# Attention state chained from PSUM, the first batch's norm in another order, and wider filler matmuls in a Trainium2 kernel

## The chip, the cores and the metric

The kernel runs on one core of one Trainium2 chip, as one launch. The metric is the device time of the launch in microseconds: the median of three runs of the kernel before is 517.42 us (517.26 to 517.53). Inside the core the engines work side by side: TensorE (PE in the profile; PEld is its loading of weights), VectorE (DVE), ScalarE (ACT), GpSimd (POOL), and SyncE (SP), which here issues DMA transfers. Each engine works through its own list of instructions in order; semaphores between them hold an instruction back until its inputs are there and its outputs' buffers are free.

## The reference

What is computed, for q, k, v, alpha of shape [4, 8, 768, 48] and two weight matrices, w_ch1 of 384x1536 and w_ch2 of 1536x384, all in float32:

```
for t in range(768):                       # per batch and head; state is 48x48
    state = alpha[t][:, None] * state + outer(k[t], v[t])
    y[t]  = q[t] @ state
x  = y of all heads side by side            # [4, 768, 384]
u  = x + real(fft(fft(x, axis=1), axis=2))  # over the sequence, then the channels
un = (u - mean(u)) / sqrt(var(u) + 1e-6)    # over the 384 channels
out = u + relu(un @ w_ch1) @ w_ch2
```

## The kernel before

One Python function, `gla_mix_ffn`, writes the whole program. It does not issue instructions at once: every call on V (VectorE), A (ScalarE), G (GpSimd), T (TensorE) is recorded in a `Plan` together with the tiles that it reads and writes, a key (its wished place) and whether it is marked low. The planner then goes through the recorded work by list scheduling, with a table of estimated durations, and writes down for each engine one fixed order. Ready work with the smallest key goes first, and work marked low may wait for a gap. The instructions are issued in that order by `emit`, so that nearly all of them carry one line number, L538 (L542 in the changed kernel); the ReLU carries L221 (L223).

The work comes in four batches. A batch has four **head pairs**, two heads side by side on 112 partitions (48 of the one, a gap, 48 of the other, which begins at `GRP` = 64). `attn_stages` writes each pair in eight stages. s1 turns alpha into running products within blocks of 128 tokens by two scans on VectorE (tiles `al`, `w`), s2 and s3 multiply k and q by them, s4 transposes k, s5 makes the masked product of q and k of each block (copied from PSUM by ScalarE, masked by GpSimd). **s6 makes the state that enters each block**: five TensorE products of k and v into one PSUM tile `pu` (five blocks of 96 columns), a multiplication of all 480 columns by `mh` on VectorE, which scales each block and zeroes the quarters that mix two heads, and then four chained `scalar_tensor_tensor` steps in the SBUF tile `tt`, each of them the state before times a factor `mt` plus the new block. `mh` comes from two ScalarE operations on `mt` and a half mask `hm`. s7 adds what the state gives to each block's output, s8 combines the blocks of tokens into `z` for the FFT.

`mix_stages` makes the two DFTs as matmuls: `mk_s(0..3)` over the sequence, `mk_d(0..2)` over the channels, each `mk_d` adding its result to one third of the first half of `u` (`us[0]`), and `fb` adding the same results, in mirrored order, to the second half (`us[1]`), whose rows `f0` has fetched in reversed order. `norm_stages` n1 computes mean and variance by `bn_stats` and `bn_aggr`, the root on ScalarE, one step of refinement on VectorE (tiles `r`), and scales on ScalarE; n2 transposes the result on TensorE and splits it into a high and a low part `x`. `ffn_stages` computes both products as three matmuls each (high by high, high by low, low by high), into `h` and then into the output. The weights are split in the same way by `wsplit(j)`, which loads a block and passes it through ScalarE, VectorE and GpSimd; `WS` names the scratch tile of each pair of blocks.

Attention and mixing of batch 0 come first, and there is no FFN to do beside them. Later the FFN of one batch runs beside the attention and mixing of the next one. Where the planner sees TensorE idle before a planned time of 120 us, it puts **filler matmuls** on a tile of zeros there, one for each 0.11 us of the gap; they write to a part of PSUM that nothing reads (L1251; a 32-column product of 32 rows). Both parts of a filler, weight load and matmul, stand in the profile; one filler makes two matmul records.

## Time and profile before

| | before |
|---|---|
| median of three runs | 517.42 us (517.26 to 517.53) |
| profiled execution, its own time | 517.73 us |
| its span | 516.0 us |
| TensorE busy | 501.2 us, 97% |
| of that, filler matmuls | 29.5 us, 696 records |
| VectorE busy | 334.8 us, 65% |
| ScalarE busy | 196.1 us, 38% |
| GpSimd busy | 65.6 us, 13% |

The profile shows one execution. The 1.7 us between span and time lie around the profiled program. A row of the timeline gives the start in us, the length, the engine, the line, the operation with the tile that it writes and those that it reads, the shapes, a count of instructions taken together, and in brackets how long the engine was idle before it and what released it. A row of the windows gives for a stretch its length and then the busy time of each engine with the count of instructions, and at the end the granted TensorE clock (1.00 is full speed), the busy share of the DMA engines and GB/s. Times of a group of matmuls reach to the end of the last one.

### The profile page before, as it was taken

How to read it: one execution, taken by the hardware profiler on the slowest of the kernel's cores; microseconds unless marked ns; L12 is line 12 of the kernel's file. 1: busy time of each engine (PE TensorE's matmuls, PEld its weight loads, DVE VectorE, ACT ScalarE, POOL GpSimd, SP SyncE). 2: the span in 40 equal slices, each digit the busy share in tenths (PEclk: the TensorE clock that was granted, in tenths of full speed). 3: DMA queues.
4: the chain of work that ended last, by engine and by line, in shares of the span. 5: the costliest groups of instructions: out<-in, count | busy, mean ns of one | idle time of the engine just before them, and what ended most of it. 6: DMA issues, size and time to landing. Idle time of an engine off the chain costs nothing.

```text
span 516.0 us, 9708 instructions
## 1 busy us (share of the span) xinstructions
PE 501.2 (97%) x3970; PEld 481.4 (93%) x3970; DVE 334.8 (65%) x729; ACT 196.1 (38%) x427; POOL 65.6 (13%) x86
## 2 busy tenths in 40 slices
PE   7999979999999999999999999999999999999995
PEld 7899868999999999999999999999999999999994
DVE  8889997997889996757799514656758213113112
ACT  4675467645663235443323214433123213111110
POOL 0312243022122000221100001112110000000000
PEclk9999998999999999999999999999999999999998
DMA  8990420422555101352431001120111001001001
GB/s 303 409 402 36 125 62 2 153 93 86 198 188 163 62 1 46 109 184 89 146 94 47 2 0 47 34 75 2 60 34 46 1 1 46 1 0 47 0 1 51
DMA packets 16978, 44.48 MB, mean 86 GB/s; under 512 B 1888, under 2 KB 7136, under 8 KB 16928
## 3 DMA queue, kind: packets, MB, share of 16 engines
q1 hardware_dynamic: 15872, 41.38, 22.5%
q0 software_dynamic: 768, 2.36, 1.6%
q8 instruction: 33, 0.54, 0.4%
q14 instruction: 17, 0.14, 0.1%
q10 hardware_dynamic: 288, 0.07, 0.1%
HBM read 36.72 MB, written 7.08 MB: 85 GB/s over the span
## 4 chain that ended last, share of the span: by engine, by line
PE 93%; DVE 3%; ACT 2%; issue 0%; ACTq 0%; DVEq 0%
PE f L538 63%; PE a L538 26%; PE f L1251 4%; DVE z L538 1%; DVE wt L538 1%; ACT wt L538 1%; ACT L538 0%; DVE y L538 0%; DVE r L538 0%; DVE f L538 0%; ACT x L538 0%; ACTq L538 0%; DVE w L538 0%; ACT b L538 0%; ACT f L538 0%
## 5 line engine op out<-in xcount | busy, mean ns | idle before, releaser
L538 PE MATMUL f<-wt,h 128*128 128x384 f32 x864 | 180.1, 344 | 0.3 <-ACT h L221 0.3
L538 PE MATMUL f<-x,wt 128*128 128x384 f32 x864 | 179.5, 345 | 0.0
L538 PEld LDWEIGHTS f<-x,wt 128*128 128x128 f32 x864 | 151.6, 189 | 1.3 <-issue 0.2
L538 PEld LDWEIGHTS f<-wt,h 128*128 128x128 f32 x864 | 150.7, 188 | 1.7 <-ACT h L221 0.4
L538 DVE SCALAR_TENSOR_TENSOR h<-f,h 128x384 fp32r<-128x384 f32 x96 | 53.2, 555 | 118.0 <-ACT h L221 117.2
L221 ACT ACTIVATE h<-f 128x384 fp32r<-128x384 f32 x96 | 47.0, 491 | 174.8 <-PE f L538 174.5
L538 POOL TENSOR_SCALAR_AFFINE_SELECT w<-w 128x384 f32<-128x384 f32 x48 | 30.1, 648 | 205.1 <-ACT w L538 143.3
L538 PE MATMUL a<-vn,w 128*128 128x64 f32 x288 | 41.2, 266 | 0.0
L538 ACT COPY w<-a 128x384 f32<-128x384 f32 (+4 forms) x60 | 26.6, 482 | 34.8 <-PE a L538 34.4
L538 PEld LDWEIGHTS a<-vn,w 128*128 128x128 f32 x288 | 39.4, 191 | 0.0
L1251 PEld LDWEIGHTS f<-zero 128*32 128x32 f32 x696 | 26.3, 119 | 7.7 <-ACT zero L538 3.3
L1251 PE MATMUL f<-zero 128*32 128x32 f32 x696 | 29.5, 203 | 3.8 <-ACT zero L538 3.3
L538 DVE TENSOR_TENSOR_SCAN w<-al,d 112x768 f32<-112x768 f32 (+1 forms) x17 | 28.4, 1670 | 4.8 <-PE a L538 4.7
L538 DVE TENSOR_TENSOR_SCAN al<-al,back 112x768 f32<-112x768 f32 (+1 forms) x17 | 28.2, 1660 | 0.0
L538 PE MATMUL a<-tt,w 112*128 112x96 f32 x144 | 28.0, 278 | 0.0
L538 PE MATMUL a<-w,al 48*128 48x128 f32 (+1 forms) x306 | 26.2, 290 | 0.0
L538 PEld LDWEIGHTS a<-w,al 48*128 48x128 f32 (+1 forms) x306 | 20.5, 187 | 5.1 <-issue 2.2
L538 PEld LDWEIGHTS a<-tt,w 112*128 112x128 f32 x144 | 23.4, 190 | 0.9
L538 DVE TENSOR_TENSOR y<-y,f 128x384 f32<-128x384 f32 (+2 forms) x36 | 18.5, 528 | 7.7 <-PE f L538 7.6
L538 DVE TENSOR_TENSOR y<-y,a 128x191 f32<-128x191 f32 (+5 forms) x66 | 21.0, 363 | 1.2 <-PE a L538 1.2
L538 ACT ACTIVATE c<-al,cm 128x781 uint8<-128x781 uint8 (+1 forms) x17 | 15.5, 912 | 14.7 <-DMA al<-in_chunked_dram 14.6
L538 DVE TENSOR_TENSOR z<-f 128x288 f32<-128x288 f32 (+3 forms) x40 | 21.1, 569 | 0.0
(120 smaller groups left out, 555.7 us busy)
## 6 DMA issues: line engine op xcount, KB each, us to landing
kq<-in_kq_dram SPq DMA_DIRECT2D x13, 768.0 KB, 6.0
wt<-in_w_dram SPq DMA_DIRECT2D x8, 768.0 KB, 7.9
al<-in_chunked_dram SPq DMA_DIRECT2D x15, 392.0 KB, 5.2
out_dram<-y SPq DMA_DIRECT2D x24, 192.0 KB, 1.9
vn<-in_v_dram SPq DMA_DIRECT2D x14, 296.0 KB, 3.7
wt<-in_w_dram SPq DMA_DIRECT2D x8, 384.0 KB, 7.2
scr<-y SPq DMA_DIRECT2D x4, 576.0 KB, 3.7
wt<-in_kq_dram SPq DMA_DIRECT2D x2, 768.0 KB, 10.0
```

Of the source, the lines that this page charges most:

```text
L221: return lambda out, x: e.activation(out, x, AF.Relu)
L538: op.ins = op.fns[op.engine](*[real(a) for a in op.args], **{k: real(x) for k, x in op.kwargs.items()})
L1251: plan.idle = (lambda: nc.tensor.matmul(warm[2][0:32, 480:512], zero.real(), zero.real(), start=True, stop=True), 1.0, WARM, ("f2", 2))
```

## The change

The change has four parts.

1. **State (s6).** The chain reads PSUM itself. ScalarE copies block 0 of `pu` to the new tile `tq`; each of the four `scalar_tensor_tensor` steps on VectorE computes the state before times `mt` plus a block of `pu`, into one of three places of `tq`. For each of the five blocks two ScalarE operations of 48x48, one for each head, write the state times `mt` to `tt`, the tile that TensorE reads. The quarters of `tt` that mix two heads are set to zero once, at the start, by GpSimd. `mh`, `hm`, the mask operations and the multiplication of 480 columns are gone.
2. **Norm of batch 0.** In batch 0 the norm of the first half is recorded ahead of `fb`, which is marked low there, as is the norm of the second half. The norm of the first half is made in two groups, thirds 0 and 1 together and third 2 alone. In all batches the refinement has fewer operations: the 1e-6 is added inside a `scalar_tensor_tensor`, and a `tensor_scalar` is replaced by such an operation as well.
3. **Fillers.** A planned gap of over 3.0 us is filled with matmuls of 128 columns, one for each 0.25 us; a shorter gap as before.
4. **Scratch.** The list `WS` now names wt6 to wt11 once each and then, in turn, `f` and `z`; `z` is taken when a batch first writes it. The splits 12 to 16 are recorded behind the first norm, with those from 18 on.

```diff
-WS = ('wt6', 'wt7', 'wt8', 'wt6', 'wt7', 'wt8', 'wt9', 'wt10', 'wt11', 'f', 'f', 'f')
+WS = ('wt6', 'wt7', 'wt8', 'wt9', 'wt10', 'wt11', 'f', 'z', 'f', 'z', 'f', 'z')
+FB0 = 11
-DUMMY = 0.11
+DUMMY = (0.11, 0.25)
+LONG = 3.0
...
-                for _ in range(int((t - max(clock["PE"], self.idle[1])) / DUMMY)):
-                    order.append(self.idle[0])
+                gap = t - max(clock["PE"], self.idle[1])
+                kind = gap > LONG
+                for _ in range(int(gap / DUMMY[kind])):
+                    order.append(self.idle[0][kind])
...
-            mh = mhs[i]
-            for hd in range(2):
-                A.activation(mh[0:CW, :, hd], mt[0:CW, 0 : NT - 1], AF.Copy, scale=hm[0:CW, hd : hd + 1])
-            V.tensor_tensor(
-                out=tt[0:CW], in0=pu[0:CW, 0 : (NT - 1) * 2 * D].rearrange("p (a h e) -> p a h e", h=2, e=D),
-                in1=mh[0:CW, :, :, None].broadcast_to([CW, NT - 1, 2, D]), op=ALU.mult,
-            )
-            for a in range(1, NT - 1):
-                V.scalar_tensor_tensor(
-                    out=tt[0:CW, a], in0=tt[0:CW, a - 1], scalar=mt[0:CW, a : a + 1], in1=tt[0:CW, a], op0=ALU.mult, op1=ALU.add,
-                )
+            past = None
+            for a in range(NT - 1):
+                now = pu[0:CW, a * 2 * D : (a + 1) * 2 * D]
+                if a:
+                    to = tq[0:CW, a % 3]
+                    V.scalar_tensor_tensor(out=to, in0=past, scalar=mt[0:CW, a - 1 : a], in1=now, op0=ALU.mult, op1=ALU.add)
+                    now = past = to
+                else:
+                    past = tq[0:CW, 0]
+                    A.copy(past, now)
+                for hd, r in ((0, slice(0, D)), (1, slice(GRP, CW))):
+                    A.activation(tt[r, a, hd], now[r, hd * D : (hd + 1) * D], AF.Copy, scale=mt[r, a : a + 1])
...
+            def scales(m0, m1):
+                for m in range(m0, m1):
+                    V.bn_stats(out=st[:, m], in_=u[:, m])
+                    V.bn_aggr(out=mv[:, m], in_=st[:, m])
+                mean, var, s, r, n = mv[:, m0:m1, 0], mv[:, m0:m1, 1], sq[:, m0:m1], r0[:, m0:m1], nm[:, m0:m1]
+                A.activation(s, var, AF.Sqrt, bias=ceps)
+                V.reciprocal(r, s)
+                V.tensor_mul(s, r, r)
+                V.scalar_tensor_tensor(out=s, in0=var, scalar=1e-6, in1=s, op0=ALU.add, op1=ALU.mult)
+                V.scalar_tensor_tensor(out=s, in0=s, scalar=0.5, in1=r, op0=ALU.mult, op1=ALU.mult)
+                V.scalar_tensor_tensor(out=r, in0=r, scalar=1.5, in1=s, op0=ALU.mult, op1=ALU.subtract)
+                V.scalar_tensor_tensor(out=n, in0=mean, scalar=-1.0, in1=r, op0=ALU.mult, op1=ALU.mult)
+                for m in range(m0, m1):
+                    A.activation(un[m], u[:, m], AF.Identity, bias=nm[:, m : m + 1], scale=r0[:, m : m + 1])
...
-            return st[:-1] + nst[:FB] + st[-1:] + nst[FB:]
+            return st[:-1] + nst + st[-1:] if b == 0 else st[:-1] + nst[:FB] + st[-1:] + nst[FB:]
...
+        short = lambda: nc.tensor.matmul(warm[2][0:32, 480:512], zero.real(), zero.real(), start=True, stop=True)
+        wide = zero[:, 0:1].broadcast_to([P, P])
+        long = lambda: nc.tensor.matmul(warm[2][0:32, 384:512], zero.real(), wide.real(), start=True, stop=True)
```

Since the planner decides the order, three places show what moved. In a tile's name the numbers behind it tell one use from the next.

VectorE at the state of pair 0, beside the scans of pair 1 (both scans stand as SCALAR_TENSOR_TENSOR here, on `al` and `d` and on `al` and `back`). Before:

```order
L538 SCALAR_TENSOR_TENSOR w_1_2_67<-al_36_101,d_136 112x768
L538 RECIPROCAL back<-w_1_2_67 112x6
L538 RECIPROCAL rec<-w_1_2_67 112x6
L538 TENSOR_TENSOR mt_134<-w_1_2_67 112x5
L538 SCALAR_TENSOR_TENSOR al_36_101<-al_36_101,back 112x768
L538 TENSOR_TENSOR tt_129<-f_0_48_113,mh_131 112x480
L538 TENSOR_TENSOR w_1_2_67<-w_1_2_67,rec 112x6x64
L538 SCALAR_TENSOR_TENSOR tt_129<-tt_129,mt_133 112x96
```

Changed:

```order
L542 SCALAR_TENSOR_TENSOR w_1_2_67<-al_36_101,d_135 112x768
L542 SCALAR_TENSOR_TENSOR tq<-tq,mt_132,f_0_48_113 112x96
L542 RECIPROCAL back<-w_1_2_67 112x6
L542 SCALAR_TENSOR_TENSOR tq<-tq,mt_132,f_0_48_113 112x96
L542 RECIPROCAL rec<-w_1_2_67 112x6
L542 SCALAR_TENSOR_TENSOR tq<-tq,mt_132,f_0_48_113 112x96
L542 TENSOR_TENSOR mt_133<-w_1_2_67 112x5
L542 SCALAR_TENSOR_TENSOR al_36_101<-al_36_101,back 112x768
L542 SCALAR_TENSOR_TENSOR tq<-tq,mt_132,f_0_48_113 112x96
```

The wide multiplication, which stood behind the second scan of pair 1, is gone, and three of the four steps of the chain now stand ahead of that scan.

VectorE at the norm of the first half of batch 0 (`y_18` is the first half of `u`, `y_20` the second; `f_0`, `f_1` and `a` are results of the second DFT). Before:

```order
L538 BN_STATS st_25_90<-y_18_83 128x6
L538 TENSOR_TENSOR y_20_85<-y_20_85,f_1_125_914 128x2
L538 BN_AGGR mv_27_92<-st_25_90 128x2
L538 TENSOR_TENSOR y_20_85<-y_20_85,f_1_125_914 128x382
L538 TENSOR_SCALAR r_0_29_94<-mv_27_92 128x3
L538 BN_STATS st_26_91<-y_20_85 128x6
L538 RECIPROCAL r_2_31_96<-r_1_30_95 128x3
L538 BN_AGGR mv_28_93<-st_26_91 128x2
L538 TENSOR_TENSOR r_1_30_95<-r_2_31_96 128x3
L538 TENSOR_TENSOR y_20_85<-y_20_85,f_0_129_937 128x2
L538 TENSOR_TENSOR r_1_30_95<-r_1_30_95,r_0_29_94 128x3
L538 TENSOR_TENSOR y_20_85<-y_20_85,f_0_129_937 128x382
```

Changed:

```order
L542 BN_STATS st_25_90<-y_18_83 128x6
L542 RECIPROCAL r_1_30_95<-r_0_29_94 128x2
L542 BN_AGGR mv_27_92<-st_25_90 128x2
L542 TENSOR_TENSOR r_0_29_94<-r_1_30_95 128x2
L542 SCALAR_TENSOR_TENSOR r_0_29_94<-mv_27_92,r_0_29_94 128x2
L542 SCALAR_TENSOR_TENSOR r_0_29_94<-r_0_29_94,r_1_30_95 128x2
L542 RECIPROCAL r_1_30_95<-r_0_29_94 128x1
L542 SCALAR_TENSOR_TENSOR r_1_30_95<-r_1_30_95,r_0_29_94 128x2
L542 TENSOR_TENSOR r_0_29_94<-r_1_30_95 128x1
L542 SCALAR_TENSOR_TENSOR r_2_31_96<-mv_27_92,r_1_30_95 128x2
```

Adds to the second half and its statistics stood between the operations of the norm; in the changed order they follow behind the norm, and the two groups of the norm are interleaved.

ScalarE ahead of that norm (`b` and `wt` are blocks of weights in splitting; the root needs the ACT_TABLE_LOAD ahead of it). Before:

```order
L538 ACTIVATE wt_0_123_909<-b_0_126_917 128x768
L538 ACTIVATE wt_0_120_894<-wt_0_120_894 128x768
L538 ACTIVATE b_0_130_941<-wt_0_56_121 128x768
L538 ACTIVATE wt_0_131_947<-b_0_130_941 128x768
L538 ACT_TABLE_LOAD
L538 ACTIVATE r_1_30_95<-mv_27_92,ceps 128x3
L538 CAST wt_0_132_959<-wt_0_120_894 128x2x384
L538 ACTIVATE f_133_974<-y_18_83,r_0_29_94,r_2_31_96 128x384 x3
```

Changed:

```order
L542 ACTIVATE b_0_133_865<-wt_0_124_825 128x768
L542 ACTIVATE wt_0_111_683<-wt_0_111_683 128x768
L542 CAST wt_0_137_887<-wt_0_109_661 128x2x384
L542 ACT_TABLE_LOAD
L542 ACTIVATE r_0_29_94<-mv_27_92,ceps 128x2
L542 ACTIVATE r_0_29_94<-mv_27_92,ceps 128x1
L542 CAST wt_0_138_902<-wt_0_111_683 128x2x384
L542 ACTIVATE f_139_910<-y_18_83,r_2_31_96,r_1_30_95 128x384 x3
L542 ACTIVATE c_0_141_940,bad<-al_135_869,cm_139 128x781
```

Ahead of the table load now stand a read of a weight block of the third group of loads (`wt_0_124`) and a cast that reads what GpSimd has multiplied (`wt_0_109`); behind the scaling stands the check of a later pair's alpha (`c`). The order of GpSimd at the same place was subtract, multiply, subtract, multiply, multiply; now two multiplications and two subtractions follow each other. On TensorE the 58 fillers at the start have become 25 wide ones, the 60 ahead of the first DFT 26 wide ones, and the 58 between the second DFT and the norm's transposes 17 wide ones; 13 more wide ones lie in the attention of pair 3.

More of the change, by code (lines that the diff above doesn't have):

```diff
@@ L613, in gla_mix_ffn @@
     tts = [fixed([P, NT - 1, 2, D], f"tt{i}") for i in range(2)]
-    mhs = [fixed([P, NT - 1, 2], f"mh{i}") for i in range(2)]
+    tq = fixed([P, 3, 2 * D], "tq")
     mts = [fixed([P, NT], f"mt{i}") for i in range(3)]
@@ L623, in gla_mix_ffn @@
     ones = fixed([P, 1], "ones")
-    hm = fixed([P, 2], "hm")
     rows = fixed([P, 3], "rows", I32)
@@ L674, in setup @@
         V.memset(zero, 0.0)
[L675 to L677 removed]
+        for x in tts:
+            G.memset(x, 0.0)
         V.memset(d1, 0.0)
@@ L852, in s8 @@
         def s8():
-            yts, zt = mixed()[0:2]
+            yts, zs = mixed()[0:2]
             first = MERGE[b].index(hp) if hp in MERGE[b] else -1
             if first >= 0:
+                if not zs:
+                    zs.append(plan.tile("z"))
+                zt = zs[0]
                 c0 = (MERGE[b][first - 1] + 1 if first else 0) * 2 * D
@@ L1043, in n1 @@
                 un = [uw[0][:, 0:DM], uw[0][:, DM:S], uw[1][:, 0:DM]]
-            V.scalar_tensor_tensor(out=vr, in0=mv[:, :, 0], scalar=-1.0, in1=r0, op0=ALU.mult, op1=ALU.mult)
-            for m in range(3):
-                A.activation(un[m], u[:, m], AF.Identity, bias=vr[:, m : m + 1], scale=r0[:, m : m + 1])
+            for m0, m1 in ((0, 2), (2, 3)) if split and blk == 0 else ((0, 3),):
+                scales(m0, m1)
             e["un"] = un
@@ L1125, in mixed @@
             if b not in sequence:
-                sequence[b] = ([plan.tile("y") for _ in range(2)], plan.tile("z"), [])
+                sequence[b] = ([plan.tile("y") for _ in range(2)], [], [])
             return sequence[b]
@@ L1191, in extra @@
             load_weights(2 + LG.index(i))
-            if i == LG[0]:
-                plan.key = KW2
-                for j in range(12, 18, 2):
-                    wsplit(j)
             plan.key = key
@@ L1211, in gla_mix_ffn @@
     for i, f in enumerate(mixing()):
+        plan.low = i == FB0
         write([f], KF0 + 0.01 * i)
+        plan.low = False
         n = MIX[i] if i < len(MIX) else 0
@@ L1221, in gla_mix_ffn @@
         sf = store_for(out[b])
-        write(norm_stages(us, 1, ress[1]), b * 1000 + KN if b else KN0)
+        plan.low = b == 0
+        write(norm_stages(us, 1, ress[1], b == 0), b * 1000 + KN if b else KN0)
+        plan.low = False
         if b == 0:
             plan.key = KW2
-            for j in range(18, NW, 2):
+            for j in range(12, NW, 2):
                 wsplit(j)
@@ L1250, in gla_mix_ffn @@
     if WARM:
-        plan.idle = (lambda: nc.tensor.matmul(warm[2][0:32, 480:512], zero.real(), zero.real(), start=True, stop=True), 1.0, WARM, ("f2", 2))
+        short = lambda: nc.tensor.matmul(warm[2][0:32, 480:512], zero.real(), zero.real(), start=True, stop=True)
+        wide = zero[:, 0:1].broadcast_to([P, P])
+        long = lambda: nc.tensor.matmul(warm[2][0:32, 384:512], zero.real(), wide.real(), start=True, stop=True)
+        plan.idle = ((short, long), 1.0, WARM, ("f2", 2))
     with tc.manual_schedule():
```

27 lines of the change are left out of this document (7 added, 20 removed).

## The prediction

> **What bounds the kernel now.** I read the page's shares first, then the windows of the whole run, then TensorE's waits. The page, TensorE's waits (line, releaser, total, times, longest) and the busy time by stretch of the span:
>
> ```profile
> PE 501.2 (97%) x3970; PEld 481.4 (93%) x3970; DVE 334.8 (65%) x729; ACT 196.1 (38%) x427; POOL 65.6 (13%) x86
> L1251 PE MATMUL f<-zero 128*32 128x32 f32 x696 | 29.5, 203 | 3.8 <-ACT zero L538 3.3
> ...
> PE f L1251 <- ACT zero L538: 3.3, 1, 3.3
> PE f L538 <- ACT f L538: 3.0, 1, 3.0
> PE f L538 <- DVE z L538: 1.3, 1, 1.3
> ...
> 85.50:508.00 422.50, 422.15 (x2866) 410.18 (x2865) 259.12 (x558) 146.32 (x326) 44.25 (x59) 1.00 0.19 63
> 60.00:70.00 10.00, 10.00 (x116) 9.06 (x115) 10.00 (x23) 8.24 (x12) 4.62 (x3) 1.00 0.14 41
> 70.00:80.00 10.00, 7.04 (x104) 5.39 (x100) 8.79 (x28) 6.05 (x11) 1.80 (x1) 0.77 0.26 80
> 160.00:200.00 40.00, 40.00 (x254) 38.76 (x253) 37.84 (x95) 14.94 (x34) 3.12 (x3) 1.00 0.21 66
> ```
>
> TensorE (PE) is busy 97% of the span, but two parts lie behind that share. From 85.5 us to 508 it idles 0.35 us in 422.5, at granted clock 1.00: there it alone sets the pace, and since the change adds and removes no matmul of the computation, that stretch keeps its length. Before it, 29.5 us of "busy" are fillers on the tile `zero`, which delay nobody but each other. So the end is the moment at which TensorE enters its unbroken stretch, plus a constant, and only what moves that moment counts. I take it as 85.81, the first matmul of the second FFN product. Batch 0 runs alone ahead of it: attention until `z` is made, the two DFTs, the norm, transposes, FFN. The profiled execution took 517.73 us: 516.0 of span and 1.7 around it, 0.3 above the median of 517.42.
>
> **The change, term 1: the state of attention in batch 0.** TensorE from its first filler, VectorE at the first two pairs, and ScalarE's work for a mask:
>
> ```profile
> 3.30 5.43 PE L1251 MATMUL f<-zero 128*32 128x32 f32 x116 [3.30 <-ACT zero L538]
> 8.66 0.51 PE L538 MATMUL a<-cst,al 112*128 112x112 f32 x3
> ...
> 13.22 0.63 PE L538 MATMUL f<-vn,kt 128*112 128x96 f32 x4
> 65.93 2.45 PE L538 MATMUL f<-cst,x 95*128 95x192 f32 x14
> ...
> 12.45 1.76 DVE L538 TENSOR_TENSOR_SCAN al<-al,back 112x768 f32<-112x768 f32 x1
> 14.13 0.63 DVE L538 TENSOR_TENSOR tt<-f,mh 112x480 f32<-112x480 f32 x1
> ...
> 20.00 0.28 DVE L538 SCALAR_TENSOR_TENSOR tt<-tt,mt 112x96 f32<-112x96 f32 x1
> 25.05 0.66 DVE L538 TENSOR_TENSOR tt<-a,mh 112x480 f32<-112x480 f32 x1 [2.35 <-PE a L538]
> 34.62 0.66 DVE L538 TENSOR_TENSOR tt<-a,mh 112x480 f32<-112x480 f32 x1 [2.22 <-PE a L538]
> 41.98 2.35 DVE L538 TENSOR_TENSOR f<-y,y 128x864 f32<-128x864 f32 x2 [1.13 <-ACT y L538]
> ...
> L538 ACT ACTIVATE mh<-mt,hm 112x5 f32<-112x5 f32 x32 | 8.4, 300 | 4.8 <-DVE mt L538 3.6 <-DVE tt L538 1.2
> ```
>
> Removed per pair: the 480-wide multiply (0.63 to 0.66 on VectorE) and two mask operations on ScalarE (0.30 each). Added per pair: one copy and ten 48x48 masks on ScalarE. I have no row for a 48x48 mask; the 112x5 row, smaller still, took 0.30 with its fixed part, and back to back such operations start closer than they last, so 0.2 to 0.3 each: ScalarE gains 11 x 0.2 to 0.3 less 0.6, 1.6 to 2.7 us a pair. The four chained steps stay (0.28 each), now reading PSUM. So VectorE saves 4 x 0.63 = 2.5 us in batch 0, and its three waits of 2.35, 2.22 and 1.13 (5.7 us) are what a different order may release. Two things count against it. The chain is now ahead of pair 1's second scan in VectorE's order, and its third and fourth steps need the state matmuls of 13.22. That scan started at 12.45 and would start near 16, 3.5 us late, with two later pairs behind it. And each state goes VectorE, ScalarE, TensorE, one hop more. Upper bound of the gain: 2.5 plus about half a microsecond of released waits, 3.0. Lower bound: the 3.5 us delay less the 2.5 saved, a loss of 1.0. I take 1.3, a little over the middle, since the waits of pairs 1 to 3 shorten the most where VectorE reaches the next pair earlier.
>
> The fillers at the start come into the same term. 58 short ones (116 records) give way to 25 wide ones, 32x128. A matmul of 192 columns took 2.45 / 7 = 0.35 in the DFT row (14 records are 7 matmuls), so a wide filler costs about 0.35 x 128/192 = 0.23. Ahead of that TensorE is slow; TensorE alone in two half-microseconds:
>
> ```profile
> 6.50:7.00 0.50, 0.50 (x14) 1.00 0.97 388
> 7.50:8.00 0.50, 0.50 (x22) 1.00 1.07 390
> ```
>
> It ran 14 records in half a microsecond up to about 7, and 22 after it. At 14/22 of the rate a wide one takes 0.37, so ten fit until 7.0 and the other 15 end near 10.5, where the short ones ended at 8.7. The first transposes of batch 0 are thus up to 1.8 us late; they waited for nothing else, but VectorE's scans, which start on their own loads, cover most of it. That is inside the range of -1.0 to 3.0.
>
> **Term 2: from `z` to the first transposes of the norm.** `z` ends where VectorE turns to the weights at 60.34:
>
> ```profile
> 60.34 1.82 DVE L538 TENSOR_TENSOR wt<-wt,wt 128x768 fp32r<-128x768 f32 x2
> 68.51 0.54 DVE L538 TENSOR_TENSOR y<-y,f 128x384 f32<-128x384 f32 x1
> 71.97 1.64 DVE L538 TENSOR_SCALAR r<-r 128x3 f32<-128x3 f32 x1
> 76.70 0.16 DVE L538 TENSOR_TENSOR r<-r 128x3 f32<-128x3 f32 x1
> 76.90 0.16 DVE L538 TENSOR_TENSOR r<-r,r 128x3 f32<-128x3 f32 x1
> ...
> 71.78 1.80 POOL L538 TENSOR_TENSOR wt<-wt,wt 128x768 fp32r<-128x768 f32 x1 [1.93 <-ACT wt L538]
> ...
> 69.39 1.28 ACT L538 ACT_TABLE_LOAD   x1
> 74.37 1.91 ACT L538 ACTIVATE f<-y,r,r 128x384 f32<-128x384 f32 x3 [2.66 <-DVE r L538]
> ...
> 75.13 0.63 PE L538 MATMUL f<-cst,f 128*128 128x128 f32 x3 [2.96 <-ACT f L538]
> wt<-in_w_dram SPq DMA_DIRECT2D x8, 768.0 KB, 7.9
> ```
>
> Before, it takes 75.13 - 60.34 = 14.8 us. The last add into the first half ends at 69.05; 6.1 us then go into a norm whose small operations follow each other at 0.20 (76.70, 76.90), because adds and statistics of the other half stand between them and because one of them took 1.64 instead of 0.16: it ran inside GpSimd's 1.80 us multiply and both ended together, at 73.6. In the new order the other half is behind. With nothing in the way: 69.05, statistics 0.6, root 0.3, six chained operations 1.2, scaling until the first transpose 0.7, is 71.85, or 11.5 after `z`: a gain of 3.2. In the way are four GpSimd operations of 1.8, now two multiplies and two subtractions back to back around the norm. And ScalarE's table load (1.28), which the root needs, now stands behind a cast that waits for the first of those multiplies, and behind a read of a weight block of the third group, whose load of 768 KB (7.9 to landing) waits for its scratch to come free. If the norm loses 1.64 once more and the root starts as late as ScalarE's scaling does now, nothing is gained. Between 0 and 3.2 I take 0.9: one lock of the two that fit, and a table load about as late as before; the six operations come out of the other half's company in any case.
>
> [...]
>
> **Term 3: transposes to the first FFN matmul.** ScalarE's check of a later pair, and the first FFN matmul:
>
> ```profile
> 45.01 0.96 ACT L538 ACTIVATE c<-al,cm 128x781 uint8<-128x781 uint8 x1
> ...
> 78.84 1.01 PE L538 MATMUL f<-x,wt 128*128 128x384 f32 x2
> ```
>
> From 75.13 to 78.84 it is 3.7 us: three groups of three transposes at half clock, with ScalarE and VectorE splitting high and low parts between. At full clock a group of 0.90 loses at most 0.45, three 1.35; one check (0.96) now stands in ScalarE's order ahead of the casts and can eat most of that. Gain 0.4 to 1.35; I take 0.65.
>
> **Term 4: the clock.** TensorE stands idle 2.96 us in front of 75.13, and then its clock is halved. TensorE alone in that stretch, and its matmuls up to the unbroken one:
>
> ```profile
> 75.50:82.00 6.50, 6.50 (x40) 0.50 0.27 104
> ...
> 68.31 3.86 PE L1251 MATMUL f<-zero 128*32 128x32 f32 x116
> ...
> 83.62 1.85 PE L538 MATMUL f<-x,wt 128*128 128x384 f32 x9
> 85.30 0.49 PE L538 MATMUL a<-cst,h 128*128 128x128 f32 x3
> ...
> 85.81 0.51 PE L538 MATMUL f<-wt,h 128*128 128x384 f32 x2
> ```
>
> The fillers at 68.31 end 2.96 before the transposes; the planned gap is filled with 17 wide ones now, 17 x 0.23 = 3.9, much what 58 short ones took, but laid to a gap that is shorter. By terms 1 and 2 the idle time left is 2.96 - 0.9 = 2.1. No row shows a drop after a wait that short: the 1.3 us wait on `z`, shortly before 60, was followed by ten microseconds at 1.00. If it holds: between 78.84 and 83.62 lie 8 FFN matmuls and 6 transposes at half clock in 4.78 us. At full clock, with 1.85 / 9 = 0.21 and 0.49 / 3 = 0.16 from the rows above, they take 8 x 0.21 + 6 x 0.16 = 2.6, or by closer packing (0.19 and 0.11) 2.2. Gain 2.2 to 2.6; taken 2.4. If the clock still drops, 0.
>
> [...]
>
> **Nothing elsewhere.** In the unbroken stretch ScalarE was busy 14.94 of 40 us; three pairs there add 3 x 2.7 = 8, and 23 is still under 40. VectorE, 37.84 of 40, loses 0.6 a pair. Without that cover the state's hop would cost 0.2 to 0.5 for each half (rival D). The scratch of the weight splits and the late norm of the second half lie under 422 us of TensorE's work.
>
> Sum: 1.3 + 0.9 + 0.65 + 2.4 = 5.25, so 517.73 - 5.25 = 512.5 profiled, 512.2 as a median.
>
> **Rivals.**
> A, the sum: 512.2, own range 510 to 514.
> B, the norm stays late: the weight read ahead of the table load, or GpSimd's lock, keeps about 2.9 us of idle time, and the clock drops again. Left are term 1 and a little of term 3, 1.6: 515.8. For it: 7.9 us of landing from an issue that can only come once the scratch is read, just after `z`, and 1.64 already seen. Against: with a DMA share of 0.26 in 70 to 80 the load has the queues nearly to itself, and 7.9 after 61 is 69, where the table load stands already.
> C, nothing is in the way: 3.0 + 3.2 + 0.65 + 2.4 = 9.25: 508.2. For it: VectorE's three waits. Against: four GpSimd operations around the norm.
> D, slower: the mask step on ScalarE, between VectorE's state and TensorE's product, sits behind FFN's own ReLUs in ScalarE's order, and TensorE waits in the unbroken stretch. Twelve pairs in two halves, at 0.5 each, are 12 us: 517.4 + 12 - 5.25 = 524. It decides from 5.25 / 24 = 0.22 a half. For it: VectorE at 37.84 of 40. Against: ScalarE's 25 idle of 40.
> E, no change: the wide fillers at the start (1.8 late) and the late scan (3.5) spend what terms 3 and 4 give: 517.
>
> **How the numbers follow.** A 0.50, B 0.20, C 0.15, D 0.08, E 0.07. The time is A's. The range holds A, C's near part and B: 507.0 to 516.5; outside lie D, E and the far end of C, 2 in 10. A measurement of this kernel tells 0.2%, 1.03 us, from no change. Faster takes A, C, and nearly all of B less some: 0.81; no change, E and a tail of B: 0.10; slower, D and a little of E: 0.09.
>
> **What would show it.** Term 1: `z` ends at 58 to 60 instead of 60.3, with the waits of 2.35 and 2.22 shortened. Term 2: first transposes 13 to 14.5 after `z`, and the new small operations not stretched to 1.6. Term 4: granted clock 1.00 in the ten microseconds around the norm, and no half-clock stretch; if the clock halves again, B is right. A wait on ScalarE of TensorE after 90, above 0.3 in all, would mean D. TensorE's count in the unbroken stretch should be the same. The prediction is wrong at its root if the distance from the first second-product matmul (85.81 before) to the end changes by more than 1 us.

## The result: 4.8 us slower

The changed kernel takes 522.31 us (median; 521.87 to 523.75) against 517.47 for the kernel before on the same chip: 1.0086 times as long, 95% interval 1.0061 to 1.0111. The forecast was 512.2, faster. The profiled execution took 523.75, with a span of 522.0 (before: 517.73 and 516.0), so the profile has 6.0 us to explain, 1.2 more than the medians differ by.

The page, TensorE's waits and the windows of the changed kernel:

```profile
PE 505.2 (97%) x3676; PEld 482.9 (93%) x3676; DVE 327.6 (63%) x709; ACT 243.3 (47%) x572; POOL 68.0 (13%) x86
...
PE f L1264 <- ACT zero L542: 3.3, 1, 3.3
PE f L542 <- ACT f L542: 3.1, 1, 3.1
PE f L542 <- DVE x L542: 1.1, 1, 1.1
PE f L1262 <- ACT x L542: 0.9, 1, 0.9
...
85.50:508.00 422.50, 420.86 (x2852) 406.77 (x2852) 252.57 (x549) 181.69 (x434) 46.29 (x57) 1.00 0.17 58
80.00:90.00 10.00, 9.12 (x50) 8.32 (x51) 7.69 (x18) 3.78 (x10) 0.00 (x0) 0.66 0.00 1
```

VectorE fell by 7.2 us, ScalarE rose by 47. The wait ahead of the norm's transposes, 2.96 before, is 3.1; the half clock (a granted clock of 0.50, from 75.5 to 82.3 before) is still there and has moved to 80.7 to 87.6; and the stretch that never waited has a new wait of 1.1 on `x`. Where the time came in shows on TensorE's own timeline, whose rows answer those that the prediction quoted:

```profile
3.30 8.49 PE L1264 MATMUL f<-zero 128*32 128x128 f32 x50 [3.30 <-ACT zero L542]
11.72 0.51 PE L542 MATMUL a<-cst,al 112*128 112x112 f32 x3
...
71.43 3.96 PE L1264 MATMUL f<-zero 128*32 128x128 f32 x34
78.47 0.55 PE L542 MATMUL f<-cst,f 128*128 128x128 f32 x3 [3.08 <-ACT f L542]
82.12 1.01 PE L542 MATMUL f<-x,wt 128*128 128x384 f32 x2
83.52 4.89 PE L542 MATMUL f<-x,wt 128*128 128x384 f32 x16
88.26 1.72 PE L542 MATMUL f<-wt,h 128*128 128x384 f32 x9
...
204.27 0.80 PE L542 MATMUL f<-x,wt 128*128 128x384 f32 x3 [1.08 <-DVE x L542]
```

| stretch (us) | before | change | difference |
|---|---|---|---|
| until the first transposes of batch 0 | 8.66 | 11.72 | +3.06 |
| from there until `z` is made | 51.76 | 51.84 | +0.08 |
| `z` to the first transposes of the norm | 14.71 | 14.91 | +0.20 |
| those to the first FFN matmul | 3.71 | 3.65 | -0.06 |
| first FFN matmul to the second product | 6.97 | 6.14 | -0.83 |
| from there to the end of the span | 430.19 | 433.74 | +3.55 |

(`z` is taken here at the end of VectorE's last operation on it, 60.42 before, 63.56 after.) The last two rows belong together: nine transposes of the second half, some 0.7 us at 0.07 to 0.08 from start to start at full clock (three from 85.30 in the kernel before, the next matmul at 85.55), stood before the second product and stand behind it now. What is left of the last row is 1.3 us of new waits (1.64 in all, against 0.34), 0.7 behind TensorE's last matmul (6.36 before, 7.07 now; 5.8 to 7.1 in the runs below), and under 1 us that no row singles out.

Two places in the rest of the profile bear on the causes. ScalarE just before `z`, in 45 to 58 us (columns as in the other windows: TensorE, weight loads, VectorE, ScalarE, GpSimd), first before, then changed, and then the new state's groups in the changed kernel:

```profile
45.00:58.00 13.00, 12.14 (x254) 11.37 (x253) 12.67 (x33) 4.46 (x9) 1.83 (x3) 1.00 0.25 79
```

```profile
45.00:58.00 13.00, 12.81 (x144) 11.75 (x144) 10.91 (x24) 12.64 (x25) 1.45 (x2) 1.00 0.03 9
...
L542 ACT ACTIVATE tt<-tq,mt 48x48 f32<-48x48 f32 x128 | 42.3, 331 | 4.5 <-DVE tq L542 2.4
L542 ACT ACTIVATE tt<-a,mt 48x48 f32<-48x48 f32 x30 | 8.9, 296 | 1.0 <-DVE tq L542 0.8
```

ScalarE went from a third busy to full: of its 12.6 us there, 3.6 are the new state's masks and copy, and about 9 are steps of the weight splits, which the planner now puts there. And VectorE beside GpSimd around the norm of the changed kernel, with ScalarE's table load and first root:

```profile
68.34 2.52 DVE L542 SCALAR_TENSOR_TENSOR wt<-wt,wt 128x768 int32<-128x768 int32 x1
74.30 1.11 DVE L542 TENSOR_TENSOR r<-r 128x2 f32<-128x2 f32 x1
75.64 1.65 DVE L542 SCALAR_TENSOR_TENSOR r<-r,r 128x2 f32<-128x2 f32 x1
...
68.22 1.82 POOL L542 TENSOR_TENSOR wt<-wt 128x768 f32<-128x768 f32 x1 [3.93 <-ACT wt L542]
71.81 1.82 POOL L542 TENSOR_TENSOR wt<-wt 128x768 f32<-128x768 f32 x1 [1.77 <-ACT wt L542]
73.58 3.69 POOL L542 TENSOR_TENSOR wt<-wt,wt 128x768 fp32r<-128x768 f32 x2
...
72.47 1.28 ACT L542 ACT_TABLE_LOAD   x1
73.77 0.29 ACT L542 ACTIVATE r<-mv,ceps 128x2 f32<-128x2 f32 x1
```

Three operations of VectorE are stretched, each inside or over an operation of GpSimd; without one of GpSimd's beside them such operations take 0.95 (from 66.07), 0.16 (from 71.23 in the kernel before) and 0.16 (from 77.32).

### The profile page after: what moved, and what is told of

It is laid out like the page before. It is cut to its first block, busy times and chain, and to the rows that moved or that the text cites. A ratio compares the mean times of both kernels' runs of the same rounds, so it can differ in the third digit from the quotient of the medians.

```text
span 522.0 us, 9288 instructions
## 1 busy us (share of the span) xinstructions
PE 505.2 (97%) x3676; PEld 482.9 (93%) x3676; DVE 327.6 (63%) x709; ACT 243.3 (47%) x572; POOL 68.0 (13%) x86
## 4 chain that ended last, share of the span: by engine, by line
PE 87%; DVE 6%; ACT 4%; issue 1%; ACTq 0%
PE f L542 59%; PE a L542 25%; PE f L1264 2%; PE f L1262 1%; DVE y L542 1%; ACT tt L542 1%; DVE wt L542 1%; DVE r L542 1%; ACT wt L542 1%; DVE z L542 1%; ACT b L542 1%; DVE w L542 1%; DVE st L542 1%; DVE al L542 0%; ACT f L542 0%
## 5 line engine op out<-in xcount | busy, mean ns | idle before, releaser
L542 POOL TENSOR_SCALAR_AFFINE_SELECT w<-w 128x384 f32<-128x384 f32 x48 | 35.7, 767 | 218.9 <-ACT w L542 161.0
L542 ACT ACTIVATE tt<-tq,mt 48x48 f32<-48x48 f32 x128 | 42.3, 331 | 4.5 <-DVE tq L542 2.4
L542 DVE SCALAR_TENSOR_TENSOR tq<-tq,mt,a 112x96 f32<-112x96 f32 x60 | 18.5, 308 | 26.4 <-ACT tt L542 25.1
L542 PE MATMUL a<-w,al 64*128 64x128 f32 (+1 forms) x306 | 26.4, 291 | 0.0
L542 PEld LDWEIGHTS a<-w,al 64*128 64x128 f32 (+1 forms) x306 | 20.7, 187 | 5.8 <-issue 2.2
L1264 PE MATMUL f<-zero 128*32 128x128 f32 x162 | 21.5, 297 | 3.3 <-ACT zero L542 3.3
L1264 PEld LDWEIGHTS f<-zero 128*32 128x32 f32 x162 | 19.2, 121 | 4.8 <-ACT zero L542 3.3
L542 DVE TENSOR_TENSOR y<-y,a 128x192 f32<-128x192 f32 (+4 forms) x66 | 21.1, 363 | 1.4 <-PE a L542 1.4
```

Of the source, the lines that this page charges most:

```text
L542: op.ins = op.fns[op.engine](*[real(a) for a in op.args], **{k: real(x) for k, x in op.kwargs.items()})
L1264: long = lambda: nc.tensor.matmul(warm[2][0:32, 384:512], zero.real(), wide.real(), start=True, stop=True)
```

## The experiments

On the chips of these runs the kernel before took 518.0 to 518.4 at the median, single runs from 516.4 to 519.7; each ratio is against the kernel before run beside it. Where two kernels are compared by their medians, the ratios give the difference up to about 1 us larger or smaller. Edits are against the change unless the text says "before".

### What the start costs

All fillers short, in the change:

```diff
-LONG = 3.0
+LONG = 1000.0
```

> The change with all fillers short, the order of everything else unchanged. Theory F (wide fillers run at the slow rate at the start, 8.49 us instead of 5.43, and hold back the first transposes, and with them all of batch 0): the first transposes come back to 8.7, z is ready 2 to 3 us earlier, the time is 519.3 (518.5 to 520.3). Theory S (the state on ScalarE is what costs, and the fillers lie in time that VectorE's scans need anyway): within 1 us of the change, 521.5 to 522.5, with z still near 63.5.

Measured: 521.52, ratio 1.0071 (1.0042 to 1.0100). `z` came 2.8 us earlier, at 60.77, as theory F has it, but the time hardly moved, because the clock was halved twice. TensorE alone in that run:

```profile
59.00:66.00 7.00, 7.00 (x53) 0.76 0.65 198
75.00:88.00 13.00, 10.37 (x57) 0.61 0.01 2
```

The short fillers ran out 2.1 us before `z` and 4.2 before the norm's transposes. F's price was right for the place, its time wrong.

Wide fillers alone, in the kernel before:

```diff
-DUMMY = 0.11
+DUMMY = (0.11, 0.25)
+LONG = 3.0
...
```

> The kernel before with the wide fillers alone. Theory F: first transposes near 11.7, z about 3 us later than 60.34, time 520.4 (519.5 to 521). Theory S: no change, 517 to 518.

Measured: 519.44, ratio 1.0026 (1.0014 to 1.0038). First transposes at 11.18, `z` 2.5 us later, and no half clock at all: the start's loss and the clock's gain, of which the former is larger. F's direction, at half of its size.

The same with the first gap left short, so that only the later long gaps are wide:

```diff
-                kind = gap > LONG
+                kind = gap > LONG and clock["PE"] > 1.0
```

> The kernel before with wide fillers in the long gaps except the first: old norm, old state. It prices the half clock alone. By the prediction's terms 3 and 4: z at 60.3, the first FFN matmul 1.3 us after it would have stood, no half clock, 3 us less, 514.5 to 515.5. If half of that is lost again behind the entrance: 516 to 517.

Measured: 517.11, ratio 0.9976 (0.9964 to 0.9988), clock 0.998. Against the run above it is 2.3 us less, the price of the wide start. Against the kernel before it is only 1.25: the first FFN matmul follows the transposes by 2.41 instead of 3.71, just the 1.3 that term 3 gave as its upper bound, but the second product came 6.11 behind that, with ScalarE's and VectorE's splitting between, and a new wait of 0.54 on `h` behind it. That is near the second expectation, not the prediction's 3 us.

That edit (short fillers in the first gap) in the change:

> The change with short fillers in the first gap alone. If the start costs what its first transposes are late, and wide fillers keep the clock at the first DFT: first transposes 8.4 to 9.5, z near 60.8, no half clock at the first DFT, 519 to 520. If the half clock's second stretch of the all-short kernel came from elsewhere: 521 to 522, with two stretches again.

Measured: 521.59, ratio 1.0060 (1.0040 to 1.0079). First transposes 8.55, `z` 60.59, no half clock at the DFT; but ahead of the norm TensorE waited 3.3, and this time the clock stayed halved from 75 to 85.5. `z` came 3.0 us earlier than in the change, and the norm was as late behind it (15.1, against 14.9). The longer half clock cost 1.7 us more of clock, the second product came 2.0 earlier, and 0.7 of that is left at the median. The time is the second expectation's, without its two stretches.

### The norm, GpSimd and the clock

The new norm alone, in the kernel before (`n1` in two groups and with fewer operations, `fb` behind it):

```diff
...
-            return st[:-1] + nst[:FB] + st[-1:] + nst[FB:]
+            return st[:-1] + nst + st[-1:] if b == 0 else st[:-1] + nst[:FB] + st[-1:] + nst[FB:]
```

> The kernel before with the new norm alone; only 39 short fillers stand in the gap ahead of it, where 58 stood. If GpSimd's multiplications and subtractions beside the norm decide in any order: first transposes 14 to 15 after z, the clock halved again, 516.8 to 517.8. If the reordering does what was predicted when the rest stays away: 12 to 13 after z, idle time 1 to 2 us, no half clock, 512.5 to 514.5.

Measured: 516.97, ratio 0.9980 (0.9968 to 0.9992). The transposes follow `z` by 12.58 instead of 14.71: the reordering gives 2.1 us by itself. But 2.03 us of waiting, and 0.72 and 0.52 right behind, halved the clock, so 1.0 was left. Half of each expectation.

The same with the wide fillers of the change in the later gaps (`kind` as in the run that left the first gap short, scratch as before):

> The kernel before with the new norm, and wide fillers in the long gaps except the one at the start: 26 ahead of the first DFT, 17 ahead of the norm's transposes. If the terms hold where neither the start nor ScalarE is burdened: z at 60.3, transposes 12 to 13 after it, granted clock 1.00 throughout, 513 to 515 (2.1 from the norm and 2 from the clock against the kernel before). If the clock is halved by any wait of 1.5 to 2 us: 516.5 to 517.5, as with the norm alone.

Measured: 517.55, ratio 1.0003 (0.9986 to 1.0020), nine of ten runs between 516.97 and 519.93. Transposes at 12.67, no wait above 0.8, and yet:

```profile
73.09 0.55 PE L542 MATMUL f<-cst,f 128*128 128x128 f32 x3 [0.17 <-ACT f L542]
75.31 0.55 PE L542 MATMUL f<-cst,f 128*128 128x128 f32 x3 [0.72 <-ACT f L542]
76.59 0.56 PE L1264 MATMUL f<-zero 128*32 128x32 f32 x12 [0.73 <-ACT x L542]
78.46 0.38 PE L1264 MATMUL f<-zero 128*32 128x32 f32 x6 [0.76 <-DVE x L542]
78.77 4.61 PE L542 MATMUL f<-x,wt 128*128 128x384 f32 x16
...
72.37 1.95 DVE L542 SCALAR_TENSOR_TENSOR r<-r,r 128x1 f32<-128x1 f32 x2
72.50 1.81 POOL L542 TENSOR_TENSOR wt<-wt,wt 128x768 fp32r<-128x768 f32 x1 [2.52 <-ACT wt L542]
```

Four small waits, 2.4 us in all, were enough: the clock was 0.50 from 78.9 to 82.3. The second of them, 0.72, comes from GpSimd's subtraction, beside which two operations for the scales of the last third took 1.95 us where two such take 0.35 (from 77.78 in the change).

GpSimd taken out of the splits, in the change; VectorE's order up to the norm stays word for word:

```diff
-FX = {... 'wm': 'VG', 'wd': 'VG', ...}
+FX = {... 'wm': 'V', 'wd': 'V', ...}
```

> The change with every multiplication and subtraction of the weight splits on VectorE and none on GpSimd; VectorE's order up to the norm is word for word that of the change. If GpSimd's four operations hold VectorE up inside the norm (2.52, 1.11 and 1.65 us where the same forms take 0.95 and 0.16): none of the three is stretched, first transposes 12 to 12.6 after z instead of 14.9, idle time ahead of them under 1.5, no half clock, 517.5 to 519.5. If ScalarE's late weight work sets the norm: transposes 14 or more after z, 521 to 523.

Measured: 516.95, ratio 0.9986 (0.9968 to 1.0005): 5.4 us less than the change, and no slower than the kernel before. The rows that were stretched, and the transposes:

```profile
67.00 0.95 DVE L542 SCALAR_TENSOR_TENSOR wt<-wt,wt 128x768 int32<-128x768 int32 x1
71.81 0.13 DVE L542 TENSOR_TENSOR r<-r 128x2 f32<-128x2 f32 x1
72.16 0.16 DVE L542 SCALAR_TENSOR_TENSOR r<-r,r 128x2 f32<-128x2 f32 x1
...
70.08 3.74 PE L1264 MATMUL f<-zero 128*32 128x128 f32 x32
73.75 0.56 PE L542 MATMUL f<-cst,f 128*128 128x128 f32 x3
78.14 3.08 PE L542 MATMUL f<-x,wt 128*128 128x384 f32 x16
```

`z` to transposes is 11.55 instead of 14.91, the fillers reach the transposes without a gap, and the clock holds. Counted from `z`, the statistics are ready 1.0 us earlier here, `r<-r` ends 2.1 earlier, and the next operation but one, `r<-r,r`, 3.6 earlier, so the three stretches carry the difference. ScalarE's table load was not what made the norm late: in the change it ended at 73.75, and the root started at 73.77, 0.2 us behind the last statistics that it needs (73.57).

Only the half clock taken away: 12 more wide fillers ahead of the late norm, all else word for word.

```diff
-                for _ in range(int(gap / DUMMY[kind])):
+                more = 12 if kind and guess and clock["PE"] > 60.0 else 0
+                for _ in range(int(gap / DUMMY[kind]) + more):
```

> The change with 29 wide fillers instead of 17 between the second DFT and the norm's transposes, everything else word for word as in the change. If the half clock costs by itself what the prediction's term 4 took: idle time ahead of the transposes 0.3 instead of 3.1, no half clock, 18 first FFN matmuls in 4.0 us instead of 6.1, 519.8 to 520.5 against the change's 522.3. If the clock falls for another reason, or the entrance of the FFN is set by ScalarE's and VectorE's splitting at any clock: 521.5 to 522.5.

Measured: 520.28, ratio 1.0043 (1.0026 to 1.0059), as the first expectation has it:

```profile
71.28 6.63 PE L1265 MATMUL f<-zero 128*32 128x128 f32 x58
78.47 0.55 PE L543 MATMUL f<-cst,f 128*128 128x128 f32 x3 [0.56 <-ACT f L543]
82.95 3.07 PE L543 MATMUL f<-x,wt 128*128 128x384 f32 x16
```

The transposes stand at 78.47 to the hundredth as in the change; the 16 matmuls take 3.07 instead of 4.89. So the clock alone is 2.0 us of the change's time (2.2 by the ratios). The remaining 3.3 to the kernel without GpSimd's splits (3.0 by the ratios) is near the norm's 14.91 - 11.55 = 3.36. The two sizes add up within the intervals of about 1 us; that they agree more closely is luck, since the start, too, was over 1 us earlier in that kernel's profiled execution (10.34, against 11.55).

### What the new state costs

The new state alone, in the kernel before (the whole of s6 as in the change, `tt` zeroed once):

```diff
...
-            V.tensor_tensor(out=tt[0:CW], in0=pu[...], in1=mh[...], op=ALU.mult)
...
+                    V.scalar_tensor_tensor(out=to, in0=past, scalar=mt[0:CW, a - 1 : a], in1=now, op0=ALU.mult, op1=ALU.add)
...
+                    A.activation(tt[r, a, hd], now[r, hd * D : (hd + 1) * D], AF.Copy, scale=mt[r, a : a + 1])
```

> The kernel before with the new state alone (chain from PSUM, masks on ScalarE). Theory F: z within 0.7 us of 60.34, time 517 to 518, since ten masks of 0.33 each in pair 3 take back on ScalarE what VectorE saves. Theory S: z 2 to 3 us later, time 520 to 521. As predicted: z 1.3 earlier, 516.1.

Measured: 521.99, ratio 1.0075 (1.0034 to 1.0117), single runs from 518.8 to 525.6; the profiled one took 519.5. Neither theory holds. Attention got 1.3 us shorter there (9.45 to 59.90), the norm came 13.05 behind `z`, and TensorE entered the second product 4.4 us earlier than before. It was lost later, mainly at the end of batch 0's FFN, where TensorE had nothing left and waited for batch 1:

```profile
196.00 1.35 PE L538 MATMUL a<-w,al 48*128 48x128 f32 x12 [0.34 <-ACT kt L538]
198.16 0.33 PE L538 MATMUL a<-cst,f 128*128 128x128 f32 x1 [0.81 <-ACT f L538]
198.75 0.33 PE L538 MATMUL a<-cst,f 128*128 128x128 f32 x1 [0.27 <-ACT f L538]
199.71 1.57 PE L538 MATMUL a<-cst,f 128*128 128x128 f32 x7 [0.63 <-ACT w L538]
...
200.00:204.00 4.00, 4.00 (x15) 0.57 0.00 0
```

From the second product to the end it took 6.2 us longer than before: these waits are 2.05, the half clock behind them 1.7, and some 2 us no row singles out. Four of the other five executions, 520.6 to 525.6, show a lower mean clock (0.980 to 0.990); the fifth, 518.8, has 0.993 like the profiled one.

The change with the state as before (s6, `mh` and `hm` put back; the diff above the other way round):

> The change with the state as before (480-wide multiplication by mh on VectorE, chain in SBUF), all else as in the change, wide fillers at the start too. If the state on ScalarE is what costs after batch 0: no wait of TensorE near 204, idle time behind the first second-product matmul under 0.6 us instead of 1.64, batch 1's first norm transposes 3 us or more earlier than 200.2; z near 63, since the start is unchanged; 518.5 to 520.5. If the norm and the scratch of the splits cause that wait: it stays, and the time is within 1 us of 522.3.

Measured: 517.09, ratio 0.9980 (0.9969 to 0.9992): 5.2 us less than the change, more than expected. The wait at 204 is gone, as the first expectation has it; but most of it came at a place that it doesn't name, the norm, 12.65 behind `z` instead of 14.91, with no half clock behind it:

```profile
72.84 0.80 DVE L542 TENSOR_TENSOR r<-r 128x2 f32<-128x2 f32 x1
73.86 0.16 DVE L542 SCALAR_TENSOR_TENSOR r<-r,r 128x2 f32<-128x2 f32 x1
...
70.03 3.58 POOL L542 TENSOR_TENSOR wt<-wt,wt 128x768 fp32r<-128x768 f32 x2
```

Three of GpSimd's operations stand here instead of four, and they end at 73.61, one small operation into the norm, where in the change they end at 77.27 and catch three of VectorE's. The state is made well ahead of this place. How it brings GpSimd's fourth operation into the norm is not shown: with another state the planner lays the splits in another order, and between 45 and 58 ScalarE is busy 12.6 us in the change, 7.5 here, and 8.7 with the new state alone and the old scratch. So the new state does not fill ScalarE by itself, nor do the other three parts without it.

Half of the masks (five for each pair; the state of the second head is left out of the product):

```diff
-                for hd, r in ((0, slice(0, D)), (1, slice(GRP, CW))):
+                for hd, r in ((0, slice(0, D)),):
```

> The change with the masks of the first head alone, five for each pair instead of ten: the state of the second head is left out of the product. If ScalarE's masks hold up VectorE's chain: VectorE's wait on them falls from 25.6 us to under 10, the wait of TensorE near 204 is gone, 520 to 521. If what costs is where the chain stands in VectorE's order: 522 to 523, with the wait still there.

Measured: 518.26, ratio 1.0005 (0.9994 to 1.0015), 4 us less than the change and lower than both expectations. Attention of batch 0 took 49.54 from the first transposes to `z`, against 51.84, and the wait at 204 is gone. VectorE's wait on the masks, which was to fall under 10, is still 23.0: most of it lies late in the program, where VectorE has time. So in attention and near 204 the masks are the price, but that wait was the wrong place to look for it. The norm is not among what they give back:

```profile
72.00 1.65 DVE L542 SCALAR_TENSOR_TENSOR r<-mv,r 128x2 f32<-128x2 f32 x1
```

Four operations of GpSimd stand beside it here, too, its transposes come 14.52 behind `z`, and a wait of 2.11 ahead of them halved the clock.

### Whether the state costs by itself

Two remedies, each worth over 5 us, can't be a sum. Four kernels, all with a short start: GpSimd taken out of all splits, or out of the first six, each with the old and the new state.

```diff
-        FL["wm"].tensor_mul(a, a, sg)
+        (V if j < 12 else FL["wm"]).tensor_mul(a, a, sg)
```

(and the same for the subtraction: the first six splits).

Old state, no split on GpSimd:

> As the kernel with the old state and the short start, and the splits' multiplications and subtractions on VectorE. If GpSimd's work still costs the norm there: first transposes 11.5 to 12 after z instead of 12.6, 513.5 to 514.5. If VectorE, at 95 percent beside the first FFN, cannot take 1.9 us more for each split: a wait of TensorE at the end of batch 0's FFN near 195 and 516 to 518.

New state, no split on GpSimd:

> The change with short fillers in the first gap and no split on GpSimd: the same as the last kernel of the call before but for the new state. Theory L (the state costs only by setting GpSimd's work into the norm): z at 60, transposes 11.6 after it, no half clock, 514 to 515, as fast as the kernel with the old state and the short start. Theory M (ScalarE's masks have a price of their own beside the first FFN): a wait of TensorE at the end of batch 0's FFN, and 516.5 to 518.

Old state, the first six on VectorE:

> The change with the old state, short fillers in the first gap, and the first six splits' multiplications and subtractions on VectorE, the later ones where the order puts them. If GpSimd costs the norm there and VectorE has room for six splits only: first transposes 11.6 to 12.2 after z, no wait near 195, 513 to 514. If the norm is already free of GpSimd in that kernel: 514.3 as without this, or 0.5 to 1 more for VectorE's part.

New state, the first six on VectorE:

> As the one before, with the new state. Theory L: within 0.7 us of it. Theory M: 2 us or more above it, with VectorE or ScalarE late for TensorE between 140 and 205.

| splits off GpSimd | old state | new state |
|---|---|---|
| all | 518.04, 0.9990 (0.9977 to 1.0002) | 515.32, 0.9957 (0.9936 to 0.9978) |
| the first six | 518.84, 1.0016 (1.0006 to 1.0025) | 516.26, 0.9972 (0.9957 to 0.9987) |

Neither theory: with VectorE carrying the splits, the new state is 2.6 to 2.7 us faster, in both pairs (by the ratios 2.3 with the first six splits off GpSimd, 1.7 with all). Of the old state's kernels the one without GpSimd's splits came as its second expectation has it, at the wait and nearly at the time; the other missed both of its expectations by over 3 us, and no row says why. All four have the norm 11.5 to 12.2 behind `z`, at full clock, and enter the second product within 0.6 us of each other (79.9 to 80.5); they differ beside the first FFN. The windows of the two kernels without GpSimd's splits, old state first:

```profile
85.00:170.00 85.00, 85.00 (x602) 80.91 (x601) 74.08 (x127) 49.41 (x102) 17.58 (x19) 1.00 0.35 120
170.00:205.00 35.00, 33.76 (x205) 30.84 (x204) 31.18 (x77) 12.30 (x30) 0.99 (x2) 0.93 0.05 18
```

```profile
85.00:170.00 85.00, 85.00 (x609) 81.36 (x608) 73.13 (x128) 60.02 (x136) 15.32 (x19) 1.00 0.35 120
170.00:205.00 35.00, 34.66 (x225) 31.75 (x223) 31.81 (x75) 13.33 (x30) 1.18 (x2) 1.00 0.05 18
```

With the old state, TensorE waits for batch 1 at 197 (1.2 us in three pieces) and, in that execution (521.28, mean clock 0.991), loses the clock behind it; the other twelve took 516.6 to 518.3 at 0.996 to 0.998. The new state leaves 0.3. In the other pair the waits do not account for it: from the second product to the end the old state took 436.5 us with 1.2 of TensorE's waits, the new one 433.3 with 2.1. What the runs show is that the state has no fixed price: with GpSimd in the splits it cost 5.2 (7.3 between the two kernels with a short start, 521.59 and 514.30), without it gained 2.6 to 2.7. That it pays where VectorE carries the splits, since it moves work from VectorE to ScalarE, fits both pairs; how much of the 2.6 is that, and how much the new order of everything else that the planner makes for each kernel, stays open.

### A version faster than both

The old state and the short start, with the change's norm, its wide fillers elsewhere and its scratch (the edits of two runs above together):

> The change with the state as before and short fillers in the first gap alone: norm, other wide fillers and scratch as in the change. If the start's delay still counts once ScalarE is free of the masks: first transposes 8.4 to 9, z 60.4, norm transposes 12.6 after it, no half clock, 514.5 to 515.5, the fastest so far. If what is gained at the start is lost to the clock again, as in the change with its short start: 516.5 to 517.5.

Measured: 514.30, ratio 0.9929 (0.9912 to 0.9946), 3.7 us under the kernel before by that ratio, single runs from 514.1 to 515.3, as the first expectation has it:

```profile
73.10 0.55 PE L542 MATMUL f<-cst,f 128*128 128x128 f32 x3 [0.36 <-ACT f L542]
77.44 3.06 PE L542 MATMUL f<-x,wt 128*128 128x384 f32 x16
```

`z` at 60.47, transposes 12.63 behind it, TensorE's waits around the norm 1.3 us in all, clock 1.00 throughout. The start is worth 2.8 us here (517.09 to 514.30), where the clock holds behind it.

This kernel differs in one part alone from the one with the new norm and the later wide fillers (517.55, ratio 1.0003): it has the scratch and the late splits of the change, its fourth part. That part is worth 3.3 us here, 3.8 by the ratios, and the two intervals lie apart. The norm's transposes begin at the same place (73.10 and 73.09), but the scales of the last third are not held up by GpSimd, TensorE's waits fall from 2.4 to 1.3 us, the clock holds, and the second product comes at 80.34 instead of 83.22. With the new state the fourth part was not tried by itself.

## Why the prediction was wrong, step by step

The forecast was 5.25 us less, and the profile shows 6.0 more. Of these 11.25 us term 1 accounts for 4.4 (3.1 lost instead of 1.3 gained), term 2 for 1.1, term 3 for 0.6, term 4 for 1.6, and the stretch that was to keep its length for 3.55.

**What bounds the kernel** was right until 85 us and not quite behind: TensorE sets the end, but the stretch did not "keep its length". Batch 0's FFN runs out near 200, and if VectorE or ScalarE are late for batch 1, TensorE waits there: 1.1 us in the change, 2.1 with the state alone, and the clock on top. Rival D had the hop on ScalarE, but in 24 places at 0.22 and more (the 0.2 to 0.5 a half was the author's estimate, and no run shows it); the wait came in one, and in the change it is VectorE's `x` that ends it.

**Term 1** is the step that failed first. "Ten fit until 7.0 and the other 15 end near 10.5": they ended at 11.8, 8.49 us for 25, since the slow rate lasted until about 9 (7 records in the microsecond from 7, 11 in that from 9); warm, a wide filler took 5.96 / 26 = 0.23, just the estimate. "VectorE's scans cover most of it": they covered none, `z` came 3.1 late for a start 3.06 late. And the gain in attention was nought instead of 1.3 and more: masks of 0.30 and 0.33, not 0.2 to 0.3 (two of the old ones took 0.49 to 0.52 back to back, two and four of the new ones 0.60 and 1.36 to 1.38), 2.95 us a pair for all that ScalarE gained, and ScalarE full in pair 3, a window that the sum did not look at. With the state alone the gain was there as forecast (1.3), and with half of the masks it is 2.3; in the change the state's masks meet the splits in that window, which is read from the timelines and was not tried by itself.

**Term 2** took 0.9 of 0 to 3.2 and got -0.2. Both ends were right: with nothing in the way 11.5 was forecast, and 11.55 was measured three times, though there the transposes follow right behind the fillers, so that the norm may have been ready a little earlier; the case in which GpSimd holds the norm up was rival B. The prediction's "lock" is measured as an operation of VectorE that is stretched until one of GpSimd's ends: the TENSOR_SCALAR of 1.64 before ends at 73.61, GpSimd's at 73.58. In the change the TENSOR_TENSOR of 1.11 ends at 75.41, where GpSimd's next starts at 75.47, and the SCALAR_TENSOR_TENSOR of 1.65 at 77.29, GpSimd's at 77.27; without GpSimd's splits they take 0.13 and 0.16. Why they wait no run shows. Not all do: inside the same operation of GpSimd as the 1.11, a RECIPROCAL from 74.10 took 0.17 and a BN_AGGR from 74.18 0.16. The error was to count one lock and give B 0.20, though four GpSimd operations at 1.8 us make 7.2 us in which more than one operation of the norm can be caught, as the 1.11 and the 1.65 were. The prediction's own example was misread: the operation of GpSimd at 71.78 is the splits' subtraction.

**Term 3** got 0.06 for 0.65. The check of 0.93 does stand ahead of the casts, but it can have cost some 0.2 at most: in the change with the old state it stands behind them, and they still start 1.80 behind the first transposes (1.99 in the change), since they wait for TensorE, and from the transposes to the first FFN matmul it is 3.21 there. The rest, some 0.3, is the half clock, which began at 80.7 in the change (six short fillers ahead of the first FFN matmul took 0.85, and 0.57 at full clock in the change with more fillers). Its upper bound, 1.35, came true (1.30) where wide fillers stood in the kernel before.

**Term 4** had the size right, 2.0 to 2.1 measured for 2.4, and the condition wrong: the 17 wide fillers ended 11.8 us behind `z`, and the transposes came at 14.9, with 3.1 us idle again. And the 2.1 us of idle time that the sum counted on would not have been safe: a wait of 2.11 halved the clock with half of the masks, 2.03 with 0.72 behind it in the new norm alone. What happened at the norm is rival B. Rival E had the start's delay, at 1.8 us of the 3.06, but no rival had the two together.

**Nothing elsewhere** put the scratch of the splits at nothing. With the old state and a short start it is worth 3.3 us, and it changes what the norm meets of GpSimd's work.

**The marker** named as the root test, the way from the first second-product matmul to the end, moved by 3.55, but some 0.7 of that is nine transposes that only changed sides: it should have been a marker that no moved work can cross.

## What to carry to other kernels

A wait removed from one engine can be paid where that engine's work goes (ScalarE in 45 to 58: busy 4.46 us before, 12.64 in the change): look at the receiving engine in the very window, not at its mean share. Work off the critical path on GpSimd can hold VectorE's smallest operations (1.65 us for one of 0.16), so in a short chain on VectorE, place GpSimd's work by the time it ends. And a filler is part of the program: at the start it took half as long again (0.34 us for 0.23), it delays what stands behind it (first transposes 3.06 us later), and where fillers ended too early for the gap, by 3.08 us at the norm, the clock was halved all the same.

## What the runs showed of the hardware

- Ahead of 508 us the half clock came in stretches of three lengths: the clock lost in one stretch is 1.71, 3.41 or 5.12 us, that is 3.4, 6.8 or 10.2 us at 0.50 (6.8 before and in the change, 3.4 with norm and wide fillers, 10.2 in the change with a short start, 3.4 and then 10.2 in the change with short fillers).
- It came behind waits in one piece and in several: 2.96 (before), 3.08 (the change) and 2.11 (half of the masks) in one, 2.03 with 0.72 behind it (the new norm alone), and four of 0.17 to 0.76, 2.4 in all, within 5.5 us (norm and wide fillers); behind 1.3 and 1.6 in all (the fastest version, the change with more fillers) it did not come. The idle time alone doesn't decide: one wait of 1.78 did not halve it (the state alone, ahead of the first DFT), and 1.2 in three pieces did, in one execution of thirteen (the old state without GpSimd's splits).
- How much half clock a kernel gets differs from run to run. Of 114 executions of the kernel before beside the experiments, the 26 with a mean clock up to 0.988 have a median of 519.0 us, the 62 at 0.989 to 0.991 one of 518.2, and the 26 above that one of 517.1.
- With the wide fillers the first transposes came at 10.3 to 11.7, with short ones at 8.3 to 9.5 in kernels that are nearly the same up to there: how long the start is slow differs from run to run. The granted clock reads 1.00 there all the while (7 records in the microsecond from 7, 11 in that from 9, in the change).
